# A fused Fourier-mixing and GEGLU kernel: one quarter's operand transposes spread over a step and a half, and one more load counted in a written-out order

## The chip, the cores and the metric

The kernel runs on one core of a Trainium2 chip. A core has a matrix engine (TensorE, in the profile PE, with its weight loads shown apart as PEld), VectorE (DVE), ScalarE (ACT), GpSimd (POOL) and SyncE (SP), which here only issues DMAs. Each engine takes its own instructions strictly in the order in which the program wrote them; an instruction that waits holds up everything behind it on the same engine, and nothing on the others.

The metric is device microseconds for one whole execution, as the median of several runs; lower is better.

## What is computed

The reference, cut to what matters, on x of 2048 tokens by 448 features, all in float32:

```python
x = A_x
xn = layernorm(x)                                   # over the 448 features
a = einsum("bsd,ed->bse", xn, dft_hid_re)           # hidden DFT
b = einsum("bsd,ed->bse", xn, dft_hid_im)
y = einsum("ts,bse->bte", dft_seq_re, a) - einsum("ts,bse->bte", dft_seq_im, b)
h = x + y
hn = layernorm(h)
g = einsum("bsd,df->bsf", hn, w_gate)               # 448 -> 1792
u = einsum("bsd,df->bsf", hn, w_up)
out = h + einsum("bsf,fd->bsd", gelu(g) * u, w_down)
```

## The kernel before

All products are made in float16, with each float32 operand split in two halves, a high part (written by ACT) and a low part, the remainder (written by DVE). Several products are done by Strassen's scheme, for which DVE or POOL first forms sums of blocks. So most operands cost an ACT pass, a DVE pass and often a few additions before TensorE can use them.

**The DFT stage.** Sixteen token tiles of 128 go through the layer norm and the hidden DFT ("features", 22 pairs of products in `feature_mm`, L497). Then eight passes go over eight units of the sequence DFT (`seq_mm`, L616). A unit's weights are one raw tile `wr`, loaded by `seq_load` (L563, 3 buffers), split into `ws`; for six of the eight units DVE also forms `wsum` (`seq_sums`, L567) and splits it into `wss`. TensorE's order, features F and units U, is the list `slots` (L755 to L773): F0 to F3, U(0,0), F10, F11, U(0,1), F4, F5, F12, F13, F6, F7, U(0,5) and so on. The first items, up to and with F2, are written by hand (L1046 to L1104).

From F3 on (`FIRST = 3`), the orders of ACT, DVE and SP are made at build time by a list planner, `arranged()` (L994 to L1044). Every piece of side work is a `Task` (L786) with an engine, a cost in microseconds, a due time, the tasks that it comes after, a lag, and a time `begin` before which it can't start. Time zero of the plan is the start of F3 on TensorE; DVE is taken to be free at -4.1. `T[n]` is the planned start of slot n, from the costs 4.16 (F), 4.54 (a plain unit) and 4.02 (a Strassen unit). An engine that is free takes, of the tasks that can start, the one with the smallest due time; the table `SHIFT` adds a number for each kind of task to its due time, so that it mostly works as a ranking of kinds. With `HOLD = (h, d)` an engine on ACT or DVE stays idle for a task that can start within h times the cost of the one it would take, if that task is due more than d before it. A kind "N" task takes no time on any engine and only sets a time. The plan decides the order of the instructions and nothing else; on the chip each engine goes as fast as its semaphores let it.

The first three raw tiles have no load task: they are loaded at fixed places (L894 to L898), and `load = None` tells the planner that the tile is there from the start. The third of them belongs to U(0,5), whose `wsum` chain is the kind "wsum" (L907); `x_stats` of the following pairs of token tiles are "xstat" (L852), the release of the PSUM banks of F0 and F1 by DVE is "flow0" and "flow1" (L877), the banks of later tiles "fhigh", "fhighp" and "flow".

**The feed-forward stage.** `STEPS` (L1128) lists 42 steps. Steps 0 to 13 multiply all gate and up weights with the first two quarters of the tokens, 512 columns at a time; steps 14 to 27 do this for the third quarter (q = 2), 28 to 41 for the last, with the products of the down matrix between them. In a step TensorE makes three results, X, Y and Z, in PSUM (class `GateUp`, L1290): `x_close` of this step and `x_open` of the next, `y_mid`, `z_open` and `y_open` of the next, `y_close`, `z_close`. ACT copies X to Y after `x_open` (L1313), applies gelu (`c_last`, L1357, and L1327) and scales (L1318, L1332); DVE combines (L1283, L1349); POOL multiplies (`c_mul`, L1361). The two halves of a step's result, `hidden(0)` and `hidden(1)`, lie in a ring of four buffers `hid` (L1340) and go to DRAM by `store(0)` and `store(1)` (L1343) during the next step; a buffer can be written again when its store has landed.

What is done beside the products is put by hand at a place in a step: `do(t, k)` runs what was registered in `side` for step t at place k. For a step of the first half the order of the program is: load of a later step's weights (`gw_load`, SP); place 0; `x_close`, `x_open`; `c_last`, `c_mul`, `store(0)` of the step before; `y_mid`; `late_prep` (splits of the gate and up weights that were not prepared in the DFT stage, with their raw loads, L689); place 1; `down_prep` (the down matrix's splits, with its loads, L254); `store(1)` of the step before; `z_open`, `y_open`, `y_close`, `z_close`; loads for the down products (L1373); place 2; further preparation, with a store of prepared weights (L752); place 4.

The third quarter's operands are made in steps 2 to 12, in two halves j = 0 and 1 of 128 tokens each, beginning at steps 2 and 7 (table at L1472 to L1491). Both halves go through one buffer `xs` in turn. `ffn_transpose` (L334) moves an `xs` into `hops[2]` by four DMA transposes, of 8, 8, 6 and 3 blocks of 128 by 128; they are called parts 0 to 3 here. Before the change, parts 0 and 1 are issued at the end (place 4) of step 6 for j = 0 and of step 11 for j = 1, parts 2 and 3 at place 1 of steps 7 and 12, ahead of `store(1)`. The first products that read `hops[2]` are those of step 14, whose `x_open`, `z_open` and `y_open` stand in step 13: part 0 is read by `x_open` and `z_open`, part 1 by `y_open` and `y_mid`, part 2 by `x_close` and `z_close`, part 3 by `y_close`. The first ACT write of the second half into `xs` (`ffn_hi(2, 1, (0,))`) is at place 2 of step 8.

Of the kernel before, what the change touches and what calls it, by code (L numbers as in the profile page):

```python
# [33 lines left out]
def kernel(  # L34
# [299 lines left out]
    def ffn_transpose(q, j, parts):  # L334
        xs = ffn[q, j][2]
        ops, c = (hops[0], 2 * q + j) if q < 2 else (hops[q], j)
        for n in parts:
            s0, s1 = ((0, 8), (8, 16), (16, 22), (22, 25))[n]
            nc.sync.dma_start_transpose(ops[:, s0:s1, c * P : (c + 1) * P], xs[:, s0 * P : s1 * P])  # L339
# [177 lines left out]
    def is_s(u):  # L517
        return u in S_UNITS
# [42 lines left out]
    wr, wsum, ws = {}, {}, {}  # L561

    def seq_load(p, u):  # L563
        wr[p, u] = dft.tile([P, 4, 2 * P], F32, tag="wr", bufs=WR_BUFS, name=f"wr{p}_{u}")
        nc.sync.dma_start(wr[p, u], w_seq[p * N_UNIT + u])

    def seq_sums(p, u):  # L567
        r = wr[p, u]
        s = wsum[p, u] = dft.tile([P, 4, 2 * P], F32, tag="wsum", bufs=1, name=f"wsum{p}_{u}")
        V.tensor_add(s[:, 0:2], r[:, 0:1].to_broadcast([P, 2, 2 * P]), r[:, 1:3])  # L570
# [12 lines left out]
    def seq_high(p, u):  # L583
        ws[p, u] = [dft.tile([P, 2, 4, 2 * P], F16, tag="ws", bufs=WS_BUFS, name=f"ws{p}_{u}")]
        for t, dst, src in seq_parts(p, u):
            hi_part(t[:, 0, dst], src, D_SC)

    def seq_low(p, u):
        for t, dst, src in seq_parts(p, u):
            lo_part(t[:, 1, dst], src, t[:, 0, dst], D_SC)  # L590

    def seq_high_s(p, u):
        t = dft.tile([P, 2, 4, 2 * P], F16, tag="wss", bufs=WSS_BUFS, name=f"wss{p}_{u}")
        ws[p, u].append(t)
        hi_part(t[:, 0], wsum[p, u], D_SC)

    def seq_low_s(p, u):
        t = ws[p, u][1]
        lo_part(t[:, 1], wsum[p, u], t[:, 0], D_SC)
# [43 lines left out]
    def h_tile(p):  # L643
        hp[divmod(p, 2)] = pair_tile(f"hx{p}")
        nc.sync.dma_start(hp[divmod(p, 2)], xr[p // 4, p % 4])
# [36 lines left out]
    class Weights:  # L682


        def __init__(self, f, pool, w_of):
            self.f, self.pool, self.w_of, self.stage = f, pool, w_of, {}
            self.raw = pool.tile([P, 2, 6, P], F32, tag="raw", name=f"gu_raw{f}")
            for r in range(2):
                nc.sync.dma_start(self.raw[:, r], w_gu[f, :, r])  # L689
# [92 lines left out]
    def plan(n, rank, *what):  # L782
        at(todo, n, *((rank, w) for w in what))


    class Task:  # L786
        def __init__(self, engine, cost, due, what, after=(), begin=-4.0, lag=0.15, kind=None):
            self.engine, self.cost, self.due, self.what = engine, cost, due + SHIFT.get(kind, 0.0), what
            self.after, self.begin, self.lag, self.kind = [t for t in after if t], begin, lag, kind
            self.end = None  # L790

    SHIFT = {"copy": 2053.2, "fhigh": -2061.7, "fhighp": -497.0, "flow0": -50.7, "flow1": -3218.4,
        "flow2": -293.1, "flow3": -1947.8, "fsum": -1010.4, "guhi": 120.6, "gulo": 604.5, "guraw": 1485.9,
        "gus1": 2529.5, "gus2": 198.7, "gwf": -5161.0, "hbias": -707.2, "hhi": -3959.1, "hlo": -461.4,
        "hload": 2567.2, "hnorm": -5834.5, "hroot": 2362.4, "hrstd": 194.6, "hsum": 70.3, "htr": 1078.2,
        "mom": 2667.7, "out": 206.3, "seed": -360.6, "shigh": -1106.1, "slow": -1267.7, "stage": -2869.5,
        "store": 2201.0, "whigh": 1230.8, "whigh0": -451.3, "whigh_s": -5463.4, "wload": 1009.0, "wlow":
        184.5, "wlow0": 106.7, "wlow_s": -2946.5, "wsum": 71.2, "xbias": -1311.5, "xbias0": -618.0, "xlo":
        -1874.4, "xlo0": -1193.9, "xload": -4441.1, "xnorm": -983.5, "xnorm0": -2048.4, "xroot": -2970.1,
        "xroot0": -522.3, "xrstd": -1046.1, "xrstd0": -708.7, "xstat": 208.5, "xstat0": -557.7, "xturn":  # L800
        481.0}
    HOLD = (0.18, 92.1)
    FIRST = 3
    COST = {"F": 4.16, "P": 4.54, "S": 4.02}
    spans = [COST["F" if s[0] == "F" else "S" if is_s(s[2]) else "P"] for s in slots]
# [3 lines left out]
    def add(*args, **kw):  # L809
        tasks.append(Task(*args, **kw))  # L810
        return tasks[-1]
# [3 lines left out]
    def chain(engine, costs, due, make, after=(), kind=None):  # L815

        run, last = [], list(after)

        def step(first):
            if first:  # L820
                run.append(make())
            next(run[0])

        for k, cost in enumerate(costs):
            on, cost = cost if isinstance(cost, tuple) else (engine, cost)
            last = [add(on, cost, due, lambda k=k: step(k == 0), after=last, kind=kind)]
        return last[0]
# [65 lines left out]
    for g, (p, u) in enumerate(units):  # L893
        n = where["U", p, u]  # L894
        if g < WR_BUFS:
            if g:
                plan((-5, 1, 2)[g - 1], 9, lambda p=p, u=u: seq_load(p, u))
            load = None  # L898
        else:
            load = add("SP", 1.7, T[n] - 12.0, lambda p=p, u=u: seq_load(p, u), after=done_with[g - WR_BUFS], lag=2.9, kind="wload")  # L900
        room = [steps[where["U", *units[g - WS_BUFS]]]] if g >= WS_BUFS else []
        size = 0.82 if is_s(u) else 1.0
        high = add("A", size, T[n] - 1.6 if g else -20.0, lambda p=p, u=u: seq_high(p, u), begin=-4.0, after=[load] + room, kind="whigh" if g else "whigh0")
        low = add("V", 0.87 if is_s(u) else 1.16, T[n] - 0.4 if g else -20.0, lambda p=p, u=u: seq_low(p, u), after=[high], kind="wlow" if g else "wlow0")
        done_with[g] = [low]
        if is_s(u):
            t = chain("V", (0.6, 0.34, 0.34), T[n] - 3.0, lambda p=p, u=u: seq_sums(p, u), [load] + sums_of, kind="wsum")  # L907
            room = [steps[s_units[-WSS_BUFS]]] if len(s_units) >= WSS_BUFS else []
            high_s = add("A", 0.98, T[n] - 1.5, lambda p=p, u=u: seq_high_s(p, u), after=[t, high] + room, kind="whigh_s")
            low_s = add("V", 1.16, T[n] - 0.3, lambda p=p, u=u: seq_low_s(p, u), after=[high_s], kind="wlow_s")  # L910
            sums_of = [low_s]
            done_with[g] += [low_s, t]
            s_units.append(n)
        steps[n].after += done_with[g]
# [4 lines left out]
    for p in range(N_PASS):  # L919
        q, j = divmod(p, 2)  # L920
        of_pass = [where["U", p, u] for u in range(N_UNIT)]
        n0, n = min(of_pass), max(of_pass) + 1
        load = fixed(n - 6 if p < 2 else n0 - 5, 9, "SP", 1.45, lambda p=p: h_tile(p), h_done.get(p - 4, ()), lag=4.0, kind="hload")
        if p >= 2:
            seed = add("A", 1.0, T[n0] - 1.0, lambda p=p: seq_seed(p), after=[load] + rooms[p - 2], begin=T[n0 - 3], kind="seed")
# [4 lines left out]
        copy = add("A", 0.35, t0 + 1.0, lambda p=p: seq_copy(p), after=[steps[n - 1], load] + last_e, kind="copy")  # L930
        mixed_in = chain("V", (1.4 if p < 2 else 0.32, 0.64, 0.86, 0.56), t0 + 5.0, lambda p=p: seq_out(p), [copy], kind="out")
        rooms[p] = [mixed_in]
        store = add("SP", 1.45, t0 + 6.0, lambda p=p: h_store(p), after=[mixed_in], lag=4.0, kind="store")
# [60 lines left out]
    def arranged():  # L994
# [18 lines left out]
        while len(begun) < len(everything):  # L1013
# [9 lines left out]
            t = able[e][0][2]  # L1023
            soon = [w[2].at for w in waiting[e] if e in "VA" and w[0] < now + HOLD[0] * t.cost and w[2].due + HOLD[1] < t.due]
            if soon:
# [446 lines left out]
    for j in range(2):  # L1472
        for f, k, what in (
            (0, 1, lambda j=j: ffn_norm_act(2, j, hp[2, j])),
            (0, 2, lambda j=j: ffn_sums(2, j, (0,))),
            (1, 1, lambda j=j: ffn_sums(2, j, (1,))),
            (1, 2, lambda j=j: ffn_sums(2, j, (2,))),
            (1, 2, lambda j=j: ffn_hi(2, j, (0,))),
            (2, 1, lambda j=j: ffn_sums(2, j, (3,))),
            (2, 1, lambda j=j: ffn_lo(2, j, (0,))),  # L1480
            (2, 2, lambda j=j: ffn_hi(2, j, (1,))),
            (3, 1, lambda j=j: ffn_lo(2, j, (1,))),
            (3, 2, lambda j=j: ffn_lo(2, j, (2,))),
            (4, 1, lambda j=j: ffn_lo(2, j, (3,))),
            (4, 2, lambda j=j: ffn_lo(2, j, (4,))),
            (4, 4, lambda j=j: ffn_transpose(2, j, (0,))),
            (4, 4, lambda j=j: ffn_transpose(2, j, (1,))),
            (5, 1, lambda j=j: ffn_transpose(2, j, (2,))),
            (5, 1, lambda j=j: ffn_transpose(2, j, (3,))),
        ):  # L1490
            at(side, ((2, 7)[j] + f, k), what)  # L1491

# [310 lines left out]
```

## Time and profile before

| quantity | value |
|---|---|
| median of 3 runs | 700.9 us (699.21 to 702.83) |
| the profiled execution's own time | 701.25 us |
| its span in the trace | 699.5 us |
| mean granted TensorE clock | 1.000 |
| PEld busy (weight loads) | 544.4 us, 78% |
| ACT busy | 417.0 us, 60% |
| POOL busy | 169.4 us, 24% |
| DMA packets, bytes | 95381, 138.77 MB |

The span is the time from the first to the last instruction; the execution's own time lies 1.75 us above it. Busy times are averages over stages with different limits. A timeline row gives start, duration, engine, line, operation, written tile <- read tiles, count, and in brackets how long the engine was idle before it and what it is taken to have waited for. The duration of a row with a count goes from the first start to the last end. Matmuls overlap, so the time between two starts tells more than a duration; rows of SPq are SP's DMA issues, and the transfer itself comes after. L numbers are lines of the kernel above.

### The profile page before, as it was taken

What the parts mean: (1) busy time and instruction counts of PE and PEld (TensorE: products, weight loads), DVE (VectorE), ACT (ScalarE), POOL (GpSimd) and SP (SyncE); (2) the same over time, 40 slices, a digit from 0 to 9 for tenths busy, and PEclk for the clock granted to TensorE, in tenths of its full rate; (3) what the DMA queues carried; (4) which work ended last, traced back from release to release, by engine and by line L of the source; (5) the groups of instructions that cost most, each with busy time, mean ns of one, the idle gap of its engine ahead of it and who ended that gap; (6) DMA issues with size and microseconds to landing.
All of it is one profiled execution on the core that took longest, in us unless ns stands there. A gap on an engine that the chain in (4) does not pass through costs nothing.

```text
span 699.5 us, 14552 instructions
## 1 busy us (share of the span) xinstructions
PE 691.6 (99%) x5643; PEld 544.4 (78%) x5643; DVE 585.0 (84%) x1112; ACT 417.0 (60%) x800; POOL 169.4 (24%) x198
## 2 busy tenths in 40 slices
PE   8999999999999999999999999999999999999998
PEld 5455769888888888888844444469999999999998
DVE  7899998999999999998568786686879785686786
ACT  6799765575757576676367765554645544455432
POOL 0000000000000000000034353164546473564452
PEclk9999999999999999999999999999999999999999
DMA  9464356559577687867457689986687684445301
GB/s 332 143 146 98 78 180 224 170 183 240 203 168 257 191 278 172 289 198 279 160 194 266 214 244 267 296 283 215 219 206 253 203 212 157 144 174 182 135 29 53
DMA packets 95381, 138.77 MB, mean 198 GB/s; under 512 B 42192, under 2 KB 71120, under 8 KB 95312
## 3 DMA queue, kind: packets, MB, share of 16 engines
q1 hardware_dynamic: 95312, 137.85, 63.8%
q8 instruction: 44, 0.72, 0.4%
q14 instruction: 25, 0.20, 0.1%
HBM read 100.99 MB, written 27.53 MB: 184 GB/s over the span
## 4 chain that ended last, share of the span: by engine, by line
PE 91%; DMA 4%; DVE 2%; SPq 1%; ACT 1%; issue 1%; DVEq 0%; ACTq 0%
PE acc L626 37%; PE acc_d L1213 16%; PE pY L1273 13%; PE pZ L1273 9%; PE pX L1273 9%; PE ab L505 7%; DMA wr<-in_w_seq_dram 1%; DMA x<-in_x_dram 1%; DMA hid_dram<-hid 1%; DMA xT<-xs 1%; SPq L339 1%; DVE gw L118 0%; DVE b L118 0%; DVE wd L118 0%; ACT x L426 0%
## 5 line engine op out<-in xcount | busy, mean ns | idle before, releaser
L1273 PEld LDWEIGHTS <-gw 128*128 128x128 f16 x1638 | 159.9, 98 | 76.8 <-issue 1.9
L626 PE MATMUL acc<-b,ws 128*128 128x224 f16 (+1 forms) x1248 | 187.1, 288 | 0.0
L626 PEld LDWEIGHTS <-ws 128*128 128x128 f16 x1248 | 120.7, 98 | 35.7 <-DVE ws L118 0.2
L626 PE MATMUL acc<-b,wss 128*128 128x224 f16 x1152 | 141.7, 259 | 0.0
L1213 PE MATMUL acc_d<-wd,dn_w 128*128 128x224 f16 x1050 | 115.5, 259 | 0.0
L626 PEld LDWEIGHTS <-wss 128*128 128x128 f16 x1152 | 110.8, 98 | 0.0
L1213 PEld LDWEIGHTS <-dn_w 128*128 128x128 f16 x1050 | 101.0, 98 | 1.9
L259 POOL TENSOR_TENSOR wd_s<-wd 128x448 f32<-128x448 f32 x7 | 8.8, 1261 | 379.6 <-DMA wd<-in_w_down_dram 349.8
L1273 PE MATMUL pY<-hops,gw 128*128 128x512 f16 (+1 forms) x476 | 88.8, 326 | 0.0
L112 ACT ACTIVATE ws<-wr 128x768 f16<-128x768 f32 (+1 forms) x64 | 56.8, 891 | 36.7 <-PE acc L626 31.5
L112 ACT ACTIVATE wss<-wsum 128x1024 f16<-128x1024 f32 x48 | 50.7, 1055 | 45.0 <-PE acc L626 23.8
L505 PE MATMUL ab<-wh,xT 128*128 128x448 f16 x352 | 69.0, 352 | 2.0 <-ACT sd_x L146 1.1
L118 DVE SCALAR_TENSOR_TENSOR ws<-wr,ws 128x768 f16<-128x768 f32 (+1 forms) x64 | 64.2, 1016 | 0.0
L118 DVE SCALAR_TENSOR_TENSOR wss<-wsum,wss 128x1024 f16<-128x1024 f32 x48 | 58.5, 1218 | 6.3 <-ACT wss L112 6.1
L1273 PE MATMUL pZ<-hops,gw 128*128 128x512 f16 (+1 forms) x308 | 59.4, 326 | 1.1 <-DVE c L1283 0.9
L505 PEld LDWEIGHTS <-xT 128*128 128x128 f16 x352 | 34.0, 98 | 33.9 <-issue 2.6
L1273 PE MATMUL pX<-hops,gw 128*128 128x512 f16 (+1 forms) x308 | 56.9, 326 | 0.0
L116 DVE TENSOR_TENSOR dn_w<-dn_s,dn_w 128x640 f16<-128x640 f32 x50 | 50.7, 1014 | 2.3 <-ACT dn_w L112 2.1
L1313 ACT ACTIVATE pY<-pX 128x256 f32<-128x256 f32 (+1 forms) x42 | 18.5, 441 | 49.5 <-PE pX L1273 49.5
L1204 POOL TENSOR_TENSOR hr<-hr,v 128x224 f32<-128x224 f32 x56 | 42.5, 781 | 12.3 <-ACT v L1172 11.9
L112 ACT ACTIVATE dn_w<-dn_s 128x640 f16<-128x640 f32 x50 | 36.5, 730 | 8.8 <-DVE dn_s L1386 6.2
L1332 ACT ACTIVATE u<-pY 128x256 f32<-128x256 f32 (+1 forms) x42 | 19.1, 454 | 35.6 <-PE pY L1273 35.5
(146 smaller groups left out, 984.5 us busy)
## 6 DMA issues: line engine op xcount, KB each, us to landing
wr<-in_w_seq_dram SPq DMA_DIRECT2D x64, 512.0 KB, 4.3
gw<-w_dram SPq DMA_DIRECT2D x36, 896.0 KB, 5.1
gu_raw<-in_w_gu_dram SPq DMA_DIRECT2D x28, 384.0 KB, 4.8
hid_dram<-hid SPq DMA_DIRECT2D x28, 256.0 KB, 5.0
hid_in<-hid_dram SPq DMA_DIRECT2D x28, 256.0 KB, 5.1
w_dram<-gu_p SPq DMA_DIRECT2D x24, 256.0 KB, 3.0
w_dram<-gw SPq DMA_DIRECT2D x6, 896.0 KB, 5.2
hx<-in_x_dram SPq DMA_DIRECT2D x8, 448.0 KB, 5.4
```

The source lines that it names most:

```text
L112: A.activation(dst, src, AF.Copy, scale=scale)
L116: V.tensor_sub(dst, src, hi)
L118: V.scalar_tensor_tensor(dst, src, scale, hi, op0=ALU.mult, op1=ALU.subtract)
L259: G.tensor_sub(s[:, 2:4], t[:, 0:2], t[:, 2:4])
L339: nc.sync.dma_start_transpose(ops[:, s0:s1, c * P : (c + 1) * P], xs[:, s0 * P : s1 * P])
L505: PE.matmul(feat[i][r][:, :D], xT[i][:, kx, :], w[:, kw, r * D : (r + 1) * D], start=n == 0, stop=n == 10,)
L626: PE.matmul(banks[k][:, cols], lhs, rhs, start=k not in begun, stop=stop, skip_group_check=True)
L1204: op(x, x, m)
L1213: PE.matmul(acc[k // 2][:, k % 2 * HD : (k % 2 + 1) * HD], a_of(la, a), b_of(lb, b), start=first and m == 0 and k % 2 == 0, stop=last and ...
L1273: PE.matmul(ps, w[:, wl, wa + ws, :], ops[:, m + ms, :], start=first and n == 0, stop=last and n == len(terms) - 1, skip_group_check=True,)
L1313: A.activation(self.Y, self.X, AF.Copy)
L1332: A.activation(u3, self.Y, AF.Copy, scale=SC)
```

## The change

Three things are changed, and no instruction is added or removed.

First, in the feed-forward stage part 0 of the third quarter's transposes stays where it was, at the end of steps 6 and 11. Part 1 moves to place 1 of steps 7 and 12, part 2 to place 2 and part 3 to place 4 of the same steps, so that part 1 stands between `store(0)` and `store(1)` of the step before, and parts 2 and 3 after `store(1)`.

Second, the planner of the DFT stage is told by an "N" task that the third raw tile comes at -2.8 of its clock; with the default lag of 0.15 its users can start at -2.65.

Third, all numbers in `SHIFT` and the second of `HOLD` are new, so the order of the instructions of ACT, DVE and SP in the DFT stage is another.

```diff
-    SHIFT = {"copy": 2053.2, "fhigh": -2061.7, "fhighp": -497.0, "flow0": -50.7, "flow1": -3218.4,
-        "flow2": -293.1, "flow3": -1947.8, "fsum": -1010.4, "guhi": 120.6, "gulo": 604.5, "guraw": 1485.9,
...
-        "store": 2201.0, "whigh": 1230.8, "whigh0": -451.3, "whigh_s": -5463.4, "wload": 1009.0, "wlow":
-        184.5, "wlow0": 106.7, "wlow_s": -2946.5, "wsum": 71.2, "xbias": -1311.5, "xbias0": -618.0, "xlo":
-        -1874.4, "xlo0": -1193.9, "xload": -4441.1, "xnorm": -983.5, "xnorm0": -2048.4, "xroot": -2970.1,
-        "xroot0": -522.3, "xrstd": -1046.1, "xrstd0": -708.7, "xstat": 208.5, "xstat0": -557.7, "xturn":
-        481.0}
-    HOLD = (0.18, 92.1)
+    SHIFT = {"copy": 847.8, "fhigh": -3030.6, "fhighp": -29.2, "flow0": -147.3, "flow1": -2027.3,
+        "flow2": -901.6, "flow3": -1874.6, "fsum": -1449.5, "guhi": -366.0, "gulo": 2413.6, "guraw": 746.5,
...
+        2819.8, "out": 198.7, "seed": 29.2, "shigh": -2627.1, "slow": -3050.2, "stage": -2497.4, "store":
+        3321.0, "whigh": 297.0, "whigh0": -364.7, "whigh_s": -4590.5, "wload": 351.0, "wlow": 176.0,
+        "wlow0": 40.0, "wlow_s": -1603.8, "wsum": 51.6, "xbias": -564.7, "xbias0": -1780.9, "xlo": -1774.0,
+        "xlo0": -1024.0, "xload": -5259.8, "xnorm": -1557.0, "xnorm0": -2339.4, "xroot": -3479.1, "xroot0":
+        -505.4, "xrstd": -1528.4, "xrstd0": -225.5, "xstat": 199.2, "xstat0": -540.6, "xturn": -297.5}
+    HOLD = (0.18, 102.7)
...
-            load = None
+            load = None if g < 2 else add("N", 0.0, 0.0, lambda: None, begin=-2.8)
...
             (4, 4, lambda j=j: ffn_transpose(2, j, (0,))),
-            (4, 4, lambda j=j: ffn_transpose(2, j, (1,))),
-            (5, 1, lambda j=j: ffn_transpose(2, j, (2,))),
-            (5, 1, lambda j=j: ffn_transpose(2, j, (3,))),
+            (5, 1, lambda j=j: ffn_transpose(2, j, (1,))),
+            (5, 2, lambda j=j: ffn_transpose(2, j, (2,))),
+            (5, 4, lambda j=j: ffn_transpose(2, j, (3,))),
```

More of the change, by code (lines that the diff above doesn't have):

```diff
@@ L790, in __init__ @@
             self.end = None
-    SHIFT = {"copy": 2053.2, "fhigh": -2061.7, "fhighp": -497.0, "flow0": -50.7, "flow1": -3218.4,
-        "flow2": -293.1, "flow3": -1947.8, "fsum": -1010.4, "guhi": 120.6, "gulo": 604.5, "guraw": 1485.9,
-        "gus1": 2529.5, "gus2": 198.7, "gwf": -5161.0, "hbias": -707.2, "hhi": -3959.1, "hlo": -461.4,
-        "hload": 2567.2, "hnorm": -5834.5, "hroot": 2362.4, "hrstd": 194.6, "hsum": 70.3, "htr": 1078.2,
-        "mom": 2667.7, "out": 206.3, "seed": -360.6, "shigh": -1106.1, "slow": -1267.7, "stage": -2869.5,
-        "store": 2201.0, "whigh": 1230.8, "whigh0": -451.3, "whigh_s": -5463.4, "wload": 1009.0, "wlow":
-        184.5, "wlow0": 106.7, "wlow_s": -2946.5, "wsum": 71.2, "xbias": -1311.5, "xbias0": -618.0, "xlo":
-        -1874.4, "xlo0": -1193.9, "xload": -4441.1, "xnorm": -983.5, "xnorm0": -2048.4, "xroot": -2970.1,
-        "xroot0": -522.3, "xrstd": -1046.1, "xrstd0": -708.7, "xstat": 208.5, "xstat0": -557.7, "xturn":
-        481.0}
-    HOLD = (0.18, 92.1)
+    SHIFT = {"copy": 847.8, "fhigh": -3030.6, "fhighp": -29.2, "flow0": -147.3, "flow1": -2027.3,
+        "flow2": -901.6, "flow3": -1874.6, "fsum": -1449.5, "guhi": -366.0, "gulo": 2413.6, "guraw": 746.5,
+        "gus1": 2878.8, "gus2": 189.7, "gwf": -5971.7, "hbias": 10.5, "hhi": -4516.3, "hlo": 86.9, "hload":
+        2580.7, "hnorm": -5754.6, "hroot": 3986.4, "hrstd": 129.2, "hsum": -273.6, "htr": 381.3, "mom":
+        2819.8, "out": 198.7, "seed": 29.2, "shigh": -2627.1, "slow": -3050.2, "stage": -2497.4, "store":
[4 more added lines that the diff above has]
+    HOLD = (0.18, 102.7)
     FIRST = 3
```

## The prediction

> **What bounds the kernel now.** I began with the page's head and the merged chain of waits.
>
> ```profile
> span 699.5 us, 14552 instructions
> PE 691.6 (99%) x5643; PEld 544.4 (78%) x5643; DVE 585.0 (84%) x1112; ACT 417.0 (60%) x800; POOL 169.4 (24%) x198
> ```
> ```profile
> 96.05 248.71 PE acc L626 x2268
> ```
>
> TensorE bounds the kernel: in the chain it follows itself for 248.71 us without a break, as it does from 33.3 us on except for what is shown below. The change takes no product away, so it can only win what TensorE stands still, and that must be found in two stretches. The first is the hand-over from the hand-written start to the planned order, in TensorE's timeline:
>
> ```profile
> 20.76 2.05 PE L505 MATMUL ab<-wh,xT 128*128 128x448 f16 x10
> 23.88 0.35 PE L505 MATMUL ab<-wh,xT 128*128 128x448 f16 x1 [1.06 <-ACT sd_x L146]
> 24.41 4.13 PE L505 MATMUL ab<-wh,xT 128*128 128x448 f16 x21 [0.18 <-DVE b L118]
> 28.38 4.70 PE L626 MATMUL acc<-b,ws 128*128 128x448 f16 x24
> 33.34 8.50 PE L505 MATMUL ab<-wh,xT 128*128 128x448 f16 x44 [0.26 <-DMA xT<-xs]
> ```
>
> One product takes (28.38 - 24.41) / 21 = 0.189 us from start to start. F3 should have begun at 20.76 + 10 x 0.189 = 22.65 and began at 23.88: 1.23 lost. Its second product should follow at 24.07 and came at 24.41: 0.34. F10 should have begun at 28.38 + 24 x 0.189 = 32.92 and began at 33.34: 0.42. The name behind the 1.06 is ACT's, but F3 writes the banks of F0, which "flow0" on DVE releases (row `b<-ab`, four pieces for F0 and F1); that row explains the 0.18 too:
>
> ```profile
> 21.35 0.69 DVE L570 TENSOR_TENSOR wsum<-wr 128x512 f32<-128x512 f32 x1 [1.36 <-DMA wr<-in_w_seq_dram]
> 21.96 1.15 DVE L379 BATCH_NORM_STATS2 st_x<-x 128x6 f32<-128x448 f32 x2
> 23.02 0.30 DVE L381 BATCH_NORM_AGGREGATE mv_x<-st_x 128x2 f32<-128x6 f32 x2
> 23.23 2.18 DVE L118 SCALAR_TENSOR_TENSOR b<-ab,b 128x448 f16<-128x448 f32 x4
> ```
>
> DVE stood still for 1.36 us, from 19.99, for the third raw tile, which the plan took to be there; the statistics and the release stood behind it.
>
> The second stretch is in the feed-forward stage. I compared the starts of TensorE's groups of X, one a step:
>
> ```profile
> 415.86 2.54 PE L1273 MATMUL pX<-hops,gw 128*128 128x512 f16 x11
> ...
> 424.28 2.54 PE L1273 MATMUL pX<-hops,gw 128*128 128x512 f16 x11
> ...
> 428.81 1.46 PE L1273 MATMUL pZ<-hops,gw 128*128 128x512 f16 x6 [0.70 <-DVE c L1283]
> ...
> 442.84 2.32 PE L1273 MATMUL pX<-hops,gw 128*128 128x512 f16 x10
> ```
>
> A free step takes 424.28 - 415.86 = 8.42; steps 9 and 10 took 18.56 instead of 16.84: 1.72 lost. They wait for DVE, and DVE waited before that for stores of the `hid` ring, which SP had issued late:
>
> ```profile
> 422.01 0.69 DVE L1283 SCALAR_TENSOR_TENSOR hid<-pZ,u 128x512 f32<-128x512 f32 x1 [2.83 <-DMA hid_dram<-hid]
> ...
> 427.47 0.69 DVE L1349 SCALAR_TENSOR_TENSOR hid<-pY,g 128x512 f32<-128x512 f32 x1 [2.23 <-DMA hid_dram<-hid]
> ```
> ```profile
> 409.03 4.42 SPq L339 DMA_TRANSPOSE hops<-xs  x2
> 413.55 0.53 SPq L1140 DMA_DIRECT2D gw<-w_dram  x1
> 414.18 1.35 SPq L1345 DMA_DIRECT2D hid_dram<-hid  x1
> 415.63 1.50 SPq L689 DMA_DIRECT2D gu_raw<-in_w_gu_dram  x2
> 417.19 3.90 SPq L339 DMA_TRANSPOSE hops<-xs  x2
> 421.13 0.58 SPq L254 DMA_DIRECT2D wd<-in_w_down_dram  x1
> 421.82 2.32 SPq L1345 DMA_DIRECT2D hid_dram<-hid  x3
> ```
> ```profile
> 411.34 1.27 POOL L1361 TENSOR_TENSOR hid<-hid,c 128x512 f32<-128x512 f32 x1 [3.57 <-ACT c L1357]
> ```
>
> SP issues back to back. `store(1)` of step 6 is ready at 412.61 (POOL's row) and goes out at 421.82; `store(0)` goes out at 414.18, and DVE gets its buffer at 422.01.
>
> So 1.23 + 0.34 + 0.42 + 1.72 = 3.71 us can be won, 0.53% of the span, just over the 0.5% (3.5 us) that a measurement of this kernel can tell from no change.
>
> **The N task, start of the DFT stage.** It issues nothing; it changes DVE's order. By the planner's rule: DVE is free at -4.10, takes the first pair's statistics (cost 1.35) and is free at -2.75. U(0,5) is slot 14, so T[14] = 4.16 + 4.54 + 2 x 4.16 + 4.54 + 6 x 4.16 = 46.52, and `wsum` was due at 46.52 - 3 + 71.2 = 114.7, before the next pair's statistics at T[2] + 208.5 = 204.3: it went first, as DVE's rows show. Now `wsum` can't start before -2.65, and DVE holds for it only if 46.52 - 3 + 51.6 + 102.7 = 197.8 is less than the statistics' -4.16 + 199.2 = 195.0. It isn't, so the statistics go at once and end at -1.40; by then flow0 can start (from -1.65, due first), and `wsum` comes behind it.
>
> On the chip that reads: statistics from 19.99 for 23.23 - 21.96 = 1.27, to 21.26; first bank free half a microsecond later (2.18 / 4 = 0.55), at 21.8, second at 22.35. TensorE wants them at 22.65 and 22.84. `wsum` follows at 22.35, after the tile landed at 21.35. Two things must be there early: ACT's part of the release, and the second pair's x tile.
>
> ```profile
> 20.00 0.98 ACT L112 ACTIVATE b<-ab 128x448 f16<-128x448 f32 x2 [3.02 <-PE ab L505]
> ```
> ```profile
> 5.90 3.66 SPq L364 DMA_DIRECT2D x<-in_x_dram  x2
> ```
> ```profile
> x<-in_x_dram SPq DMA_DIRECT2D x2, 448.0 KB, 9.4
> ```
>
> ACT is done at 20.98; the later x load was issued by 9.2 and needed about 9.4, so it is there near 18.6. The 1.57 of F3 goes, with margins of 0.85 and 0.49. What is late next is F10: TensorE wants it 1.57 earlier, while its norm, behind DVE and ACT, comes 1.36 earlier, DVE's idle time. If nothing else changes its wait grows from 0.42 to 0.63 and the start wins 1.57 - 0.21 = 1.36; if the transposes gain more, up to 1.99. I take 1.4, the end that follows from rows.
>
> **The new ranking, rest of the DFT stage.** The order of kinds stays nearly the same (on SP only `hload` and `store` swap). The work that hides it is TensorE's own; TensorE lost nothing here, so there is nothing to win, and a loss is possible only where ACT and DVE have no slack:
>
> ```profile
> 50.00:75.00 25.00, 25.00 (x153) 14.77 (x152) 23.49 (x48) 24.27 (x45) 0.00 (x0) 1.00 0.40 94
> ```
>
> ACT is busy 24.27 of 25 us and DVE 23.49. "fhigh" (banks) still ranks above "shigh", and "slow", which frees the buffers that "fhigh" needs, rises to the top of DVE's list. I take 0; from below nothing, from above see the last rival.
>
> **The transposes, half j = 0.** The same eight are issued. New order on SP from 409: part 0, `gw`, `store(0)` of step 6, two raw loads, part 1, `wd`, `store(1)` of step 6, parts 2 and 3, then the stores of step 7. `store(0)` goes out some 2.2 us earlier, one transpose of the 4.42. `store(1)` passes parts 2 and 3: 3.90 earlier, about 418; a little less if SP waits for the raw tile. Both buffers then come free before DVE wants them; DVE's two waits, 2.83 and 2.23, shrink to what ACT and TensorE set, and the combination that held TensorE at 428.81 comes at least the second wait, 2.23 us, earlier. Needed are 0.86: a step has 39 products, so one takes 8.42 / 39 = 0.216, and this group, behind 17 of them, was due at 424.28 + 17 x 0.216 = 427.95. The lesser stalls up to 442.84 are the same backlog of DVE. So 1.72 goes.
>
> What is late next is part 3. It was issued fourth and now goes behind `wd` and `store(1)` as well. ACT waited for it:
>
> ```profile
> 425.31 0.83 ACT L112 ACTIVATE xs<-xn_h 128x256 f16<-128x256 f32 x2 [2.39 <-DMA hops<-xs]
> ...
> 428.28 0.60 ACT L1327 ACTIVATE g<-pX 128x512 f32<-128x512 f32 x1 [1.31 <-DVE hid L1349]
> ```
>
> Behind that wait on ACT stand a weight split, the gelu at 428.28 and the copy of X into Y without which `y_open` can't begin; TensorE waits for those. The gelu had 1.31 us of slack after the wait, so part 3 may land about 1.2 later, by 426.5, before TensorE loses, then one for one. By SP's issue it comes 0.58 + 0.53 = 1.1 later: no loss. By bytes, `wd` and a store are 448 + 256 = 704 KB, and this stretch moved
>
> ```profile
> 400.00:430.00 30.00, 29.30 (x137) 13.14 (x135) 22.58 (x38) 18.27 (x33) 10.80 (x9) 1.00 0.98 264
> ```
>
> 264 GB/s: 2.7 us later, a loss of 1.5. SP's issue is the nearer row, since SP is back to back throughout and the weights go out earlier than before; I take a loss of 0.2. The Trainium skill ("DMA: Bandwidth & Descriptors", section "Queues, rings and completion order") says that each DMA engine consumes a queue's descriptors in ring order. By that, bytes put ahead of part 3 delay it and can't be overtaken; with the same page's 358 GB/s from HBM for a core ("Specifications") 704 KB are, as an estimate, 2.0 us, and the sum would be 0.6 us worse than mine.
>
> **Half j = 1.** Part 1 goes behind one store, part 2 behind `store(1)`, part 3 behind the weight store at the end of step 12, ahead of the next `gw` load, the `hr` load and `store(0)` of step 12.
>
> ```profile
> 453.63 2.66 SPq L339 DMA_TRANSPOSE hops<-xs  x2
> ```
> ```profile
> 463.36 1.90 PE L1273 MATMUL pY<-hops,gw 128*128 128x256 f16 x11
> ```
>
> Part 1 now goes out at about 453.6 and is first read at 463.36. In the crowded stretch above the last pair took 425.31 - 417.19 = 8.1 us from first issue to landing, so even that is in time. Parts 2 and 3 are read only within step 14, later still. Those passed on SP are a microsecond later and have a step's time. I take 0.
>
> **Sum.** 701.25 of the profiled execution (span and 1.75 around it) less 1.4 and less 1.72 - 0.2 = 1.5 gives 698.35. That execution lies 0.35 above the median of the runs, 700.9, so the forecast is 698.0.
>
> **Rivals.** First, all of it goes and F10's wait too: 700.9 - 3.7 = 697.2. For it: `ws` of U(0,0) and with it the fourth raw load come earlier and leave the queue before F10's transpose. Against: TensorE wants F10 earlier as well.
>
> Second, part 3 holds ACT and takes the place of the wait removed: 700.9 - 1.4 - 0.2 = 699.3, with the loss of 1.5. For it: the share of 0.98 in the last row of windows. This is what the ring-order rule leans to.
>
> Third, the start doesn't do what it says: DVE still has `wsum` ahead of flow0, or the statistics wait for their own tile. Then 700.9 - 1.5 = 699.4. The hold rule decides by 197.8 against 195.0, a narrow margin; against it, the same arithmetic gives the old order rightly.
>
> Fourth, slower: in the stretch from 50 to 75 us the new ranking puts a 1.45 us piece (the cost in "shigh", L869) before a bank release, so that the feature tile after next waits. It decides from three such tiles on: at 3 x 1.45 = 4.4 it outweighs 2.9. With four, 5.8: 700.9 - 2.9 + 5.8 = 703.8. For it: ACT's 97% there. Against: the ranks of these kinds.
>
> **Numbers.** Forecast 0.50 (of it a tenth measured past the bound), all of it 0.18, part 3 holds ACT 0.15, start unchanged 0.08, slower 0.09, half of that past the bound. Faster by over 0.5% (below 697.4): 0.18 + 0.05 = 0.23; slower by over 0.5% (above 704.4): 0.05; within: 0.72. The forecast's own range is 697.2 to 699.4. With the second and third rival and a microsecond for the median of runs that spread from 699.21 to 702.83, the range is 696.5 to 701.3.
>
> **What would show it.** In the changed profile: DVE's statistics directly behind each other near 19.99 with no wait for `wr`; F3 at about 22.65; a wait of F10 of 0 to 0.6; `store(1)` of step 6 about 418 minus the start's gain; steps 9 and 10 of 8.42 each; ACT's `xs` row near 425 with its wait. I am wrong on the start if F3 still waits for DVE, on the transposes if the two steps still take over 17.5 or TensorE waits there for ACT's copy, and on the ranking if TensorE shows gaps between 35 and 345 us.

## The result, and the profile after

| | before | after |
|---|---|---|
| median | 701.5 us (4 runs, 699.21 to 702.83) | 712.27 us (4 runs, 711.57 to 712.47) |
| profiled execution, own time | 701.25 us | 712.47 us |
| its span | 699.5 us | 710.7 us |
| mean granted TensorE clock | 1.000 | 0.993 |

The ratio is 1.0155, with a 95% interval of 1.0126 to 1.0184: the changed kernel is slower, by 11 us, where 698.0 was forecast and the range ended at 701.3.

Three rows of TensorE's timeline cut the span into three: the first product of F10, the first of the feed-forward stage, and the last group (start, duration, engine, line, operation, tiles, count). After:

```profile
32.20 8.50 PE L505 MATMUL ab<-wh,xT 128*128 128x448 f16 x44 [0.23 <-DMA xT<-xs]
...
357.40 1.46 PE L1272 MATMUL pX<-hops,gw 128*128 128x512 f16 x6
...
706.76 0.74 PE L1212 MATMUL acc_d<-wd,dn_w 128*128 128x224 f16 x6
```

and of before the two that the prediction didn't show:

```profile
344.60 1.46 PE L1273 MATMUL pX<-hops,gw 128*128 128x512 f16 x6
...
695.54 0.74 PE L1213 MATMUL acc_d<-wd,dn_w 128*128 128x224 f16 x6
```

Up to F10 the change wins 33.34 - 32.20 = 1.14 us. From F10 to the feed-forward stage it takes 357.40 - 32.20 = 325.20 instead of 344.60 - 33.34 = 311.26: 13.94 lost. In the feed-forward stage it takes 349.36 instead of 350.94: 1.58 won. The sum, 11.22, is the whole difference of the two profiled executions.

**The two ends did what was forecast.** The start, in TensorE's timeline and in DVE's:

```profile
21.15 6.22 PE L505 MATMUL ab<-wh,xT 128*128 128x448 f16 x32
```
```profile
19.02 1.14 DVE L379 BATCH_NORM_STATS2 st_x<-x 128x6 f32<-128x448 f32 x2
...
20.29 1.12 DVE L379 BATCH_NORM_STATS2 st_x<-x 128x6 f32<-128x448 f32 x2
...
21.54 1.12 DVE L118 SCALAR_TENSOR_TENSOR b<-ab,b 128x448 f16<-128x448 f32 x2
22.58 0.68 DVE L570 TENSOR_TENSOR wsum<-wr 128x512 f32<-128x512 f32 x1
```

The statistics stand directly behind each other, the first two bank releases `b<-ab` follow, `wsum` comes behind them, and F3 has no wait (32 products in one group). The feed-forward stage, in the timelines of TensorE, DVE, SP's issues and ACT:

```profile
437.08 2.54 PE L1272 MATMUL pX<-hops,gw 128*128 128x512 f16 x11
445.50 2.54 PE L1272 MATMUL pX<-hops,gw 128*128 128x512 f16 x11
453.92 2.54 PE L1272 MATMUL pX<-hops,gw 128*128 128x512 f16 x11
```
```profile
433.43 0.69 DVE L1282 SCALAR_TENSOR_TENSOR hid<-pZ,u 128x512 f32<-128x512 f32 x1 [1.45 <-DMA hid_dram<-hid]
438.25 0.69 DVE L1348 SCALAR_TENSOR_TENSOR hid<-pY,g 128x512 f32<-128x512 f32 x1 [1.62 <-DMA hid_dram<-hid]
```
```profile
425.58 0.55 SPq L1344 DMA_DIRECT2D hid_dram<-hid  x1
...
430.99 1.18 SPq L254 DMA_DIRECT2D wd<-in_w_down_dram  x1
432.28 0.53 SPq L1344 DMA_DIRECT2D hid_dram<-hid  x1
432.85 3.90 SPq L339 DMA_TRANSPOSE hops<-xs  x2
```
```profile
439.27 0.83 ACT L112 ACTIVATE xs<-xn_h 128x256 f16<-128x256 f32 x2 [3.55 <-DMA hops<-xs]
...
440.84 0.57 ACT L1326 ACTIVATE g<-pX 128x512 f32<-128x512 f32 x1
```

Steps 9 and 10 take 8.42 us each. `store(0)` of step 6 goes out 425.58 - 357.40 = 68.18 behind the stage's start (before: 414.18 - 344.60 = 69.58), and DVE's first wait, which is for it, is 1.45 instead of 2.83. `store(1)` goes out at 432.28 - 357.40 = 74.88 (before: 421.82 - 344.60 = 77.22), and DVE's second wait is 1.62 instead of 2.23. ACT waits longer for part 3, 3.55 instead of 2.39, but the gelu behind it starts without a wait, 83.44 behind the stage's start (before 83.68).

**The middle.** TensorE's waits and its timeline show what isn't in the profile of before at all:

```profile
PE acc L626 <- DVE ws L118: 8.6, 2, 4.9
...
PE acc L626 <- ACT acc L611: 0.6, 1, 0.6
```
```profile
178.02 2.24 PE L626 MATMUL acc<-b,ws 128*128 128x448 f16 x11 [0.56 <-ACT acc L611]
...
229.06 0.93 PE L626 MATMUL acc<-b,ws 128*128 128x224 f16 x4 [4.87 <-DVE ws L118]
...
264.80 0.62 PE L626 MATMUL acc<-b,ws 128*128 128x224 f16 x4 [3.76 <-DVE ws L118]
```

Two long stops, at U(4,4) and U(5,3), wait for the low half of the unit's weights (`ws`, kind "wlow", on DVE); a short one at U(3,0) waits for ACT's `acc`, L611. Together 0.56 + 4.87 + 3.76 = 9.19 us. The rest of the 13.94 is in the windows behind the two long stops (length, busy times with counts of PE, PEld, DVE, ACT and POOL, then the granted clock; DMA share and GB/s last):

```profile
226.00:228.00 2.00, 0.00 (x0) 0.00 (x0) 2.00 (x6) 0.77 (x2) 0.00 (x0) 0.90 0.32 65
228.00:229.00 1.00, 0.00 (x0) 0.00 (x0) 1.00 (x3) 0.00 (x0) 0.00 (x0) 0.50 0.73 133
229.00:234.00 5.00, 4.94 (x27) 4.04 (x28) 4.93 (x11) 0.00 (x0) 0.00 (x0) 0.50 0.76 232
234.00:236.00 2.00, 2.00 (x18) 1.70 (x17) 1.93 (x5) 1.16 (x2) 0.00 (x0) 0.89 1.00 265
264.00:266.00 2.00, 1.20 (x9) 1.05 (x10) 2.00 (x3) 0.32 (x1) 0.00 (x0) 0.79 0.21 41
266.00:268.00 2.00, 2.00 (x12) 1.63 (x11) 1.97 (x5) 0.02 (x1) 0.00 (x0) 0.50 0.63 215
268.00:270.00 2.00, 2.00 (x20) 1.88 (x18) 1.97 (x5) 1.13 (x3) 0.00 (x0) 0.86 0.43 149
```

TensorE is busy, but at half its clock: 5 x 0.50 + 2 x 0.11 = 2.72 and 2 x 0.21 + 2 x 0.50 + 2 x 0.14 = 1.70 us lost. 9.19 + 4.42 = 13.6 of 13.94. (The clock fell before TensorE went on at 229.06, as the first two rows show; while it stands still, the lower clock costs nothing.)

Why the low half was late is seen on ACT and DVE. ACT's high half, and DVE's list from there:

```profile
216.14 0.83 ACT L112 ACTIVATE ws<-wr 128x768 f16<-128x768 f32 x1
```
```profile
219.59 0.42 DVE L289 TENSOR_TENSOR tt<-xn_h 128x256 f32<-128x256 f32 x1
...
221.10 1.23 DVE L118 SCALAR_TENSOR_TENSOR wss<-wsum,wss 128x1024 f16<-128x1024 f32 x1 [0.23 <-ACT wss L112]
...
222.51 0.55 DVE L700 TENSOR_TENSOR gu_s<-gu_s,gu_raw 128x384 f32<-128x384 f32 x1
...
224.51 0.42 DVE L116 TENSOR_TENSOR xs<-xn_h,xs 128x256 f16<-128x256 f32 x1
...
225.18 0.95 DVE L116 TENSOR_TENSOR xs<-tt,xs 128x768 f16<-128x768 f32 x1
...
226.92 1.21 DVE L118 SCALAR_TENSOR_TENSOR wss<-wsum,wss 128x1024 f16<-128x1024 f32 x1
228.06 2.95 DVE L118 SCALAR_TENSOR_TENSOR ws<-wr,ws 128x768 f16<-128x768 f32 x3
```

The low half could start at 216.97 and starts at 228.06. Between them DVE stands still for 0.23 us only; it does sums and splits for the feed-forward stage (`tt`, `gu_s`, `xs`: that stage begins at 357) and `wsum`, `wss` of this and later units. Then three `ws` come in a row. DVE has no room for that: in the kernel before it is busy 23.24 of 25 us there too, only with the pieces in another order. There the low half of U(4,4) is done ten microseconds earlier:

```profile
217.76 0.95 DVE L118 SCALAR_TENSOR_TENSOR ws<-wr,ws 128x768 f16<-128x768 f32 x1
```
```profile
175.00:200.00 25.00, 25.00 (x217) 20.62 (x215) 24.50 (x48) 18.04 (x34) 0.00 (x0) 1.00 0.65 194
200.00:225.00 25.00, 25.00 (x240) 22.81 (x238) 23.24 (x47) 17.21 (x32) 0.00 (x0) 1.00 0.82 241
```

The planner's own numbers (`arranged()`, run by itself) say how the table does this. With the new one the low half of U(4,4) is due at 375.1, and everything that DVE takes while it is ready is due earlier: `hsum` at -102 to -99, `wsum` at 248 to 257, `hlo` at 264 to 268, `gus2` at 365.5, for instance. With the old table these kinds rank before it too (it is due at 383.6). A low half thus goes when none of them is ready, and with the new table one always was, from 199.4 to 210.2 of the plan's time.

Theory R, then: the new ranking alone makes the loss, by DVE's order, and the other two parts win about what was forecast. Rival N: the N task, or the ranking and the N task together, upset the list. Open too was whether the slow clock is an effect of the stops.

### The profile page after: what moved, and what is told of

Same layout as the page of the kernel before. It is cut to its first block, busy times and chain, and to the rows that moved or that the text cites. A ratio compares the mean times of both kernels' runs of the same rounds, so it can differ in the third digit from the quotient of the medians.

```text
span 710.7 us, 14543 instructions
## 1 busy us (share of the span) xinstructions
PE 695.3 (98%) x5643; PEld 546.6 (77%) x5643; DVE 586.7 (83%) x1112; ACT 416.0 (59%) x800; POOL 170.7 (24%) x198
## 4 chain that ended last, share of the span: by engine, by line
PE 86%; DVE 9%; ACT 3%; DMA 1%; issue 1%; SPq 0%; ACTq 0%; DVEq 0%
PE acc L626 30%; PE acc_d L1212 16%; PE pY L1272 15%; PE pZ L1272 9%; PE pX L1272 9%; PE ab L505 7%; DVE wss L118 2%; DVE xs L116 1%; DVE ws L118 1%; DVE wsum L570 1%; ACT wss L112 1%; DMA wh_raw<-in_w_hid_dram 1%; DMA xT<-xs 1%; DVE wsum L572 0%; DVE wsum L574 0%
## 5 line engine op out<-in xcount | busy, mean ns | idle before, releaser
L626 PE MATMUL acc<-b,ws 128*128 128x224 f16 (+1 forms) x1248 | 189.5, 290 | 9.2 <-DVE ws L118 8.6
L626 PE MATMUL acc<-b,wss 128*128 128x224 f16 x1152 | 144.4, 262 | 0.0
L626 PEld LDWEIGHTS <-wss 128*128 128x128 f16 x1152 | 112.3, 99 | 0.9
```

What stands on the lines that cost most here:

```text
L626: PE.matmul(banks[k][:, cols], lhs, rhs, start=k not in begun, stop=stop, skip_group_check=True)
```

## The experiments

The table gives, for each run, the three stretches cut at the same three rows as above. "To before" is the ratio to the kernel before on the same chip, with its interval; it is estimated over all runs and can differ by 0.001 from the ratio of the medians. The kernel before took 701.5 us beside the changed one, 701.24 beside e1 to e4, 700.72 beside e5 to e9 and 701.52 beside e10 and e11. The stretches and the clock are those of the profiled execution, which can lie beside the median (by 2.9 us in e7).

| run | median, us | to before | to F10 | F10 to FFN | FFN | clock |
|---|---|---|---|---|---|---|
| before | 701.24 | | 33.34 | 311.26 | 350.94 | 1.000 |
| after | 712.27 | 1.0155 [1.0126, 1.0184] | 32.20 | 325.20 | 349.36 | 0.993 |
| e1, new ranking alone | 713.41 | 1.0184 [1.0161, 1.0206] | 32.86 | 324.59 | 349.26 | 0.993 |
| e2, N task alone | 700.33 | 0.9987 [0.9975, 0.9999] | 32.39 | 311.25 | 351.47 | 1.000 |
| e3, transposes alone | 700.11 | 0.9990 [0.9980, 1.0001] | 33.42 | 311.60 | 349.29 | 1.000 |
| e4, both without the ranking | 698.95 | 0.9967 [0.9957, 0.9978] | 31.96 | 311.79 | 349.40 | 1.000 |
| e5, gus2 back | 700.54 | 0.9994 [0.9982, 1.0006] | 32.16 | 311.96 | 349.85 | 1.000 |
| e6, xrstd back | 699.08 | 0.9973 [0.9961, 0.9986] | 32.05 | 311.25 | 349.80 | 1.000 |
| e7, stops partly filled | 712.89 | 1.0172 [1.0146, 1.0197] | 32.35 | 322.48 | 349.27 | 0.997 |
| e9, two low parts first | 704.55 | 1.0051 [1.0035, 1.0066] | 32.27 | 316.22 | 349.24 | 0.999 |
| e10, stops filled | 709.34 | 1.0117 [1.0097, 1.0137] | 33.30 | 320.94 | 349.48 | 1.000 |
| e11, third ranking | 699.08 | 0.9975 [0.9962, 0.9987] | 32.84 | 311.25 | 349.49 | 1.000 |

**The three parts one by one.** e1 is the kernel before with the new `SHIFT` and `HOLD` and nothing else; e2 to e4 have the old tables and

```diff
-            load = None                                          # e2, e4
+            load = None if g < 2 else add("N", 0.0, 0.0, lambda: None, begin=-2.8)
-            (4, 4, lambda j=j: ffn_transpose(2, j, (1,))),       # e3, e4
-            (5, 1, lambda j=j: ffn_transpose(2, j, (2,))),
-            (5, 1, lambda j=j: ffn_transpose(2, j, (3,))),
+            (5, 1, lambda j=j: ffn_transpose(2, j, (1,))),
+            (5, 2, lambda j=j: ffn_transpose(2, j, (2,))),
+            (5, 4, lambda j=j: ffn_transpose(2, j, (3,))),
```

Expected of e1: 

> The kernel before with the new SHIFT and HOLD alone. Theory R (the new ranking alone makes the loss; the other two parts won what was forecast): slower than before by 13 to 15 us, since the 3.1 to 3.3 us that the other parts win in the changed kernel are missing here; TensorE stops for about 5 us near 225 us and about 4 us near 262 us, and the old stalls at F3 (1.6 us) and in steps 9 and 10 (1.7 us) are there as before. Rival N (the N task upsets the order further down): within 2 us of the kernel before, without the two long stops.

Expected of e2: 

> The kernel before with the N task alone; on DVE only the first wsum moves behind flow0, and SP, ACT and POOL keep their orders. Theory R: faster by 1.0 to 2.0 us; F3's 1.57 us gone, F10's wait 0.2 to 0.6 us, no stop of TensorE after 35 us in the DFT stage, steps 9 and 10 of the feed-forward stage still 1.7 us too long. Rival N: slower by 9 us or more.

Expected of e3: 

> The kernel before with the transposes moved and nothing else. Theory R: faster by 1.3 to 1.9 us; steps 9 and 10 take 8.42 us each, ACT's wait for the last transpose of the first half stays under the 1.2 us of slack that it had more than before. Rival (the last transpose holds ACT and takes the place of the wait removed): the two steps together still lose 0.8 to 1.5 us, and the gain is under 0.9 us.

Expected of e4: 

> The changed kernel with the old SHIFT and HOLD put back, so the N task and the moved transposes together. Theory R: faster than before by 2.5 to 3.5 us, both gains in full, and so faster than the changed kernel by about 14 us. Rival N or a joint effect: slower than before.

e1 has the whole loss, 12.9 us (11.3 to 14.4), with the same two stops; TensorE's waits there have this row:

```profile
PE acc L626 <- DVE ws L118: 8.6, 2, 4.9
```

In e2, e3 and e4 the middle takes 311.25 to 311.79 us, as before. So Rival N falls. All three gains came out below what was expected: e2 wins 0.9 us (0.1 to 1.8), e3 0.7 (-0.1 to 1.4), and e4 0.0033 x 701.24 = 2.3 us (1.5 to 3.0), so that it beats both kernels. e3's rival has the smaller gain right, but not its mechanism: in e3's trace TensorE has no wait in the feed-forward stage.

Two things in e1 were misses. F3's loss, with the order of before on DVE, was 1.0 us there and in e3, not 1.57: DVE waited 0.75 and 0.78 us for the third raw tile, where it had waited 1.36 in the profile before. And the transposes of e1 stand where they did, and yet its feed-forward stage has no stop (349.26, like the runs with the transposes moved). SP's issues there:

```profile
429.66 2.94 SPq L339 DMA_TRANSPOSE hops<-xs  x2
...
433.33 2.30 SPq L1344 DMA_DIRECT2D hid_dram<-hid  x3
```

Parts 2 and 3 held SP for 2.94 us instead of 3.90, and `store(1)` went out 433.33 - 357.45 = 75.88 behind the stage's start, not 77.22. It seems that this was enough, and that the stop of 1.72 in the profile before hung on the last microsecond or two of SP's queue. It may be absent in some runs of the kernel before too, which would explain why e3 wins 1.65 in its trace and 0.7 (-0.1 to 1.4) in its median; both are argued, not shown.

**Is it one number of the ranking?** e5 and e6 are the changed kernel with one of its 52 `SHIFT` values taken back.

```diff
-        "gus2": 189.7,            # e5
+        "gus2": 198.7,
-        "xrstd": -1528.4,         # e6
+        "xrstd": -1046.1,
```

Expected of e5: 

> The changed kernel with one entry of the ranking back at its old value: gus2 (VectorE's half of the FFN weights' split, which runs in the DFT stage) 198.7 instead of 189.7. Theory R (the ranking makes VectorE's list put the low parts of two units behind work that could wait; the two long stops and the slow clock behind them are the whole loss): in the list that the planner writes for this table the units U(4,4) and U(5,3) find their low parts in time and only U(3,0) waits; on the chip TensorE shows no gap of 4 to 5 us near 224 and 261 us, a gap of 0.7 near 177 us stays, and the time is 699 to 700.5 us, by the two stops of 5.13 and 4.02 us and some 3.7 us of slow clock less than 712.3. Rival L (something outside VectorE's order, such as a late transfer or the transposes' queue, holds the units): the stops stay, 711 to 713 us.

Expected of e6: 

> The changed kernel with another single entry back at its old value: xrstd (the reciprocal root of the x statistics, one small step of 16) -1046.1 instead of -1528.4. It has nothing to do with the low parts of the DFT units. Theory R in its strong form (the table is a set of starting values of a list schedule, and any small step can tip VectorE's order in it): the list written for this table leaves all units from U(1,3) to U(5,4) without a wait, so no long stop on the chip and 698 to 700 us. Rival K (each kind does its own harm; the harm is that of the FFN weights' split or of the sums, which stay here): the stops of 5.1 and 4.0 us stay, 711 to 713 us.

Both came out as Theory R had it: no long stop in either, and e5 keeps the short one. In e5's waits of TensorE nothing of `ws` is left:

```profile
PE acc L626 <- ACT acc L611: 0.6, 1, 0.6
...
PE pY L1272 <- ACT pY L1312: 0.3, 1, 0.3
```

So no kind is to blame: `xrstd`, a small step in the statistics of x, removes the stops as well as `gus2` does. The order as a whole is what went wrong. And it isn't the ranks that count, but the numbers: 198.7 leaves `gus2` in its place among DVE's kinds (level with `out`, its neighbour), and the list is another.

e5's time, 700.54, is just above its range of 699 to 700.5. Part of that is the last row, which belongs to the feed-forward stage: there part 3 came 426.59 - 344.12 = 82.47 behind the stage's start, later than in any other run with the transposes moved, and TensorE waited for ACT's copy of X into Y. The step took 432.71 - 423.80 = 8.91 us instead of 8.42.

**Backlog or two misplaced pieces?** e9 keeps the changed kernel's list and takes just the two low parts forward.

```diff
         low = add("V", ..., kind="wlow" if g else "wlow0")
+        low.first = n in (51, 58)
...
-        begun.sort(key=lambda t: t.start)
+        begun.sort(key=lambda t: t.at if getattr(t, "first", False) else t.start)
```

Expected: 

> The changed kernel; only the two low parts that TensorE waited for, those of U(4,4) and U(5,3), are put into VectorE's order at the point where their high parts are ready, ahead of the sums and splits that stood before them; everything else keeps its order. Theory B (backlog: VectorE has been given 4 to 5 us of work that could have waited, so by then it is behind with all the units, and putting one piece forward makes the next one late): the stops move on to the next units, U(4,1), U(4,6), U(4,7), U(5,4) and U(5,5), in smaller pieces of 1 to 3 us each, and the sum of them stays within 1.5 us; the time is 708 to 712.5 us, the lower end if the shorter stops leave the clock alone. Rival O (only two pieces stood in the wrong place): the stops go and nothing follows, 699 to 700.5 us.

TensorE's waits in e9:

```profile
PE acc L626 <- DVE ws L118: 2.6, 2, 1.5
...
PE acc L626 <- DVE wss L118: 0.9, 1, 0.9
```

704.55 lies outside both expectations. The stops move on to the next units, as Theory B said, but their sum falls from 8.6 to 2.6 + 0.9 = 3.5 us, and the clock stays up. Only DVE's order differs from the changed kernel's, so more than half of the standstill came from the place of two pieces of 0.95 us on DVE. The other 3.5 us is read here as backlog: DVE is behind with several units.

**The clock.** e7 and e10 put matmuls of 64 columns, into PSUM columns that nobody reads, into the two stops, ahead of the first product that needs the low part:

```diff
+                        if cc == 0 and (a, o, m) == (0, 0, 2):
+                            for _ in range({(4, 4): 50, (5, 3): 38}.get((p, u), 0)):    # e10: 140 and 105
+                                PE.matmul(banks[3][:, D : D + 64], w[0][:, 0, 0, 0:P], b[:, 0, 0, 0:64], ...)
```

Expected of e7: 

> The changed kernel, with 50 and 38 small extra matmuls (64 columns, into columns of a PSUM bank that nobody reads) in the units U(4,4) and U(5,3), between the matmuls that don't need the low part and the first that does: they fill most of the two long stops and change nothing else. Theory C (TensorE's granted clock falls because the engine stood still, and costs what the stops' lengths don't explain): the stops stay as waits of the same end, the granted clock is near 1 in the 5 us behind them instead of 0.50, and the time is 708 to 709 us, 3.3 to 4.3 us less than the changed kernel's 712.3. Rival W (the clock falls for another reason, or the extra time is VectorE's backlog going on): 711.5 to 713 us, and the clock falls as before.

Expected of e10: 

> As the run with small extra matmuls in the two long stops, but with 140 and 105 of them instead of 50 and 38: at the 33 ns that one took there they fill 4.6 and 3.5 us, so that TensorE stands still for 1.5 us at most. Theory C (the clock falls behind a stop of more than about 3 us, and each fall costs some 2 us): the first fall goes too, all runs have a mean clock of 0.998 or more, and the time is 707 to 709 us; the waits of the low parts end where they did. Rival W (the clock falls for another reason): some runs or all at a clock of 0.990 to 0.995 and a median of 711 us or more.

e7 was a miss for both theories. In its profiled run, of 710.04 us, the first stop is still 3.41 us long and the clock falls at its end; the second is 2.7 us long (waits 6.1 in all), and there it doesn't fall:

```profile
224.17 1.62 PE L634 MATMUL acc<-b,ws 128*128 128x64 f16 x50
229.20 0.93 PE L626 MATMUL acc<-b,ws 128*128 128x224 f16 x4 [3.41 <-DVE ws L118]
```
```profile
229.00:232.00 3.00, 2.80 (x16) 2.28 (x17) 3.00 (x6) 0.00 (x0) 0.00 (x0) 0.50 0.62 178
264.00:268.00 4.00, 4.00 (x43) 4.00 (x42) 3.96 (x8) 0.55 (x1) 0.00 (x0) 1.00 0.41 137
```

Its four runs took 710.04, 711.75, 714.04 and 714.89 us at mean clocks of 0.997, 0.995, 0.993 and 0.990. If a mean clock of c loses (1 - c) times the span, these runs without that loss are 707.8 to 709.1, so most of their spread goes with the clock. That is no general rule: e1, with the same two stops, took 712.78 us at 0.990 and 716.22 at 0.993. e10 fills nearly all of both stops, and there the clock stays at 1.00:

```profile
225.13 4.25 PE L634 MATMUL acc<-b,ws 128*128 128x64 f16 x140
230.16 0.56 PE L626 MATMUL acc<-b,ws 128*128 128x224 f16 x4 [0.78 <-DVE ws L118]
```
```profile
229.00:234.00 5.00, 4.22 (x53) 4.10 (x50) 4.96 (x10) 0.00 (x0) 0.00 (x0) 1.00 0.69 184
262.00:268.00 6.00, 5.30 (x70) 5.19 (x67) 5.93 (x13) 1.31 (x3) 0.00 (x0) 1.00 0.36 128
```

U(4,4) waits just as long for DVE (its low part is used at 230.16 here instead of 229.06, with F10 1.10 later than after's), and the middle is 325.20 - 320.94 = 4.26 us shorter, close to the 4.42 counted from the clock. The medians differ by 2.9 only, since the start of e10 lost 1.10 to F10's transpose. e10's 709.34 is thus just above Theory C's 707 to 709, and one of its five runs has a mean clock of 0.997 where 0.998 was the least expected (some runs of the kernel before, which has no such stops, show 0.997 too). The rest is as Theory C had it, and Rival W falls: a third of the loss in the middle is the price that the clock puts on standing still.

**A third ranking.** e11 has the N task and the transposes, and a table mixed from old, new and a few other values; the list that the planner writes from it has no stop of TensorE behind F10.

Expected: 

> The third part of the change and the N task as they are, with a third ranking of the kinds: old and new values mixed, and a few others, chosen so that the list which the planner writes has no stop of TensorE left from the fifth slot on (U(0,0) and F10 keep theirs of about 1 us each in the list; the changed kernel's list has five more, 13.9 us in all). Theory R (the stops in the planner's own list are those of the chip where they are long; what the old ranking leaves is under 1 us each): no gap over 0.5 us between F10 and the FFN stage, and 698.0 to 699.2 us, the same as the old ranking with the two other parts (698.95) or up to 0.9 us less. Rival P (the list is too rough a picture of the chip, which agreed only by chance): stops elsewhere, 700 us or more.

It has none on the chip, and its middle, 311.25, is that of the kernel before within 0.01. Its time, 699.08 us, is that of e4 (698.95) and e6. TensorE's waits in it, 2.8 us in all, lie in the first 34 us. This table takes back what the changed one lost and wins nothing beyond it: there was nothing to win in the middle.

## Why the prediction was wrong

The step that failed is "The new ranking, rest of the DFT stage", and in it the sentence "I take 0". It was to cost nothing and cost 13.94 us. The prediction's own test, "on the ranking if TensorE shows gaps between 35 and 345 us", decided against it. Three things in that step were wrong.

- "The order of kinds stays nearly the same" was taken for "the order of the instructions stays the same". The order of kinds decides only among tasks that are ready at the same time, and by numbers added to due times, not by ranks. e6 and e5 show how little it takes: one value of a kind that has nothing to do with the units, or one that leaves the order of DVE's kinds as it was, and both stops are gone.
- It named the condition, "a loss is possible only where ACT and DVE have no slack", and looked at one stretch, from 50 to 75 us. DVE had little further on either: 24.50 and 23.24 of 25 us busy from 175 to 225, quoted above. So it couldn't make up for a needed piece that stood 228.06 - 216.97 = 11.1 us of other work too late.
- It applied the planner's rule by hand to three tasks at the start and to none of the rest, though the rule was there. Written out in full by the planner's own code (these are its numbers, not the chip's), the changed list has TensorE stand still before U(3,0), U(4,4) and U(5,3) by 2.79, 6.00 and 4.21 in its own time; the chip showed 0.56, 4.87 and 3.76. The list from the old table has one stop of over 1.1 there, of 1.99, which the chip doesn't show. So it exaggerates, but the long stops are in it.

The fourth rival had the right part of the change and the right sign, and the wrong mechanism: not a 1.45 us piece ahead of a bank release at 50 to 75 us, but feed-forward work ahead of weight splits at 217 to 264. Its 703.8 was too low: it counted 5.8 us of waiting where 9.19 came, and no rival priced the 4.4 us at half the clock behind the waits.

The rest held. **Start:** the order on DVE came as derived from 197.8 against 195.0, and F3's 1.57 went. F10's wait is 0.23 in the row (0.26 before); the gain is 1.14 in after, 1.38 in e4 and 0.95 in e2, where F10 waits 0.76, against 1.4 forecast. Single executions scatter here: F10 begins at 32.84 and 33.30 in e11 and e10, which have the N task, and at 32.86 in e1, which hasn't.

**Transposes, j = 0:** 1.58 won in after, 1.65 in e3's trace, 1.54 in e4's, against 1.5. Part 3 "may land about 1.2 later", and that was just enough: ACT's `xs` came 439.27 - 357.40 = 81.87 behind the stage's start instead of 425.31 - 344.60 = 80.71, 1.16 later, and TensorE lost nothing. That this is the 1.1 worked out from SP's issue is luck: SP had issued parts 2 and 3 by 436.75 - 357.40 = 79.35, 2.86 later than before (421.09 - 344.60 = 76.49), and they then landed 1.7 sooner, which nothing in the prediction provides for. The slack of 1.2 was right: in e5, where the row came 82.47 - 80.71 = 1.76 later, it gives a loss of 1.76 - 1.2 = 0.56, and the step was 0.49 too long.

The price by bytes, 1.5, didn't come, and the 0.6 more by the Trainium skill ("DMA: Bandwidth & Descriptors", "Queues, rings and completion order") didn't either. That the bytes ahead can't be overtaken is also more than the section says: by it descriptors are consumed in ring order, but a later one may finish its write before an earlier one.

`store(0)` went out 1.40 earlier where 2.2 was forecast, and `store(1)` 2.34 earlier where 3.90 was, since `gw` and `wd`, ahead of them, took SP 1.45 and 1.18 instead of 0.53 and 0.58; it was still enough.

**Half j = 1:** no wait of TensorE, as said. **Their sum,** 2.9, measured 2.3 (1.5 to 3.0) in e4: without the new ranking the forecast of 698.0 would have been 1 us from the time, 698.95.

## What to carry to other kernels

When a change touches a planner's priorities, write out the whole list that it makes and go through it for the bounding engine's waits: a ranking that looks the same can give another list, and a stage where the engine that feeds the bound is busy 93 to 98% of the time, as DVE was here from 175 to 225, has no room for it. Test such a table apart from the changes that came with it, since here 2.3 us were won and 13.9 lost in one go. And price a stop of several microseconds on TensorE at more than its length: here those of 4.87 and 3.76 us cost 2.7 and 1.7 on top.

## What the hardware showed that was not expected

TensorE's granted clock fell to 0.50 in or just behind waits of 4.87, 3.76 and 3.41 us, and not at 2.7 (e7), 1.5 (e9) or 0.56. That made 4.4 of the 13.9 us lost, and in e7, whose first stop seems to be at the edge, most of a spread of 5 us between runs. In windows of 0.05 us the clock is at 0.50 from 227.62 to 234.44 and from 265.16 to 268.58 in the changed kernel, and from 229.02 to 232.43 in e7: for 6.83, 3.41 and 3.41 us, once or twice the same length. The two falls of the changed kernel lie 37.55 us apart, eleven times that length, and the second came 0.36 us after TensorE had gone on at 264.80. So the clock looks as if it were set at the ends of periods of 3.41 us that run on their own, and a period with a little work in it can still count as idle.

The Trainium skill ("TensorE: Matmul & The Clock Gate", "Part 1: The HAM clock gate (the "warmup" mystery)") says that an idle window of about 3.4 us brings half the clock, that about 3.4 us of work brings it back, and that the window runs freely, so that the moment varies from run to run. The lengths and the spacing agree with that, and so do the waits on both sides, 2.7 and 3.41. That the first stretch took two windows agrees too: TensorE stood still until 229.06, in the first of them.
